# Attention scores of a head pair in TensorE's two row halves, in an attention and MLP kernel

## The chip, the cores and the metric

One core of one Trainium2 chip runs the whole program. The metric is device time in microseconds (us), here the median of several executions. All executions quoted below are in the fast state. "Span" is that of the one execution that was profiled, from its first recorded instruction to its last; it is a little shorter than the time of the same execution (602.1 of 603.85 us in the changed kernel). A first-time reader needs four engine names: TensorE (PE, matmuls, with its weight loads as PEld), VectorE (DVE), ScalarE (ACT) and GpSimd (POOL, which here casts and issues most loads).

## The reference, cut to what matters

```python
q, k, v: (8 batches, 12 heads, 448 positions, 64) float32
q_n = q / (norm(q) + 1e-6);  k_n = k / (norm(k) + 1e-6)
attn = softmax(q_n @ k_n.T / 0.1)              # 448 x 448 per head
x = (attn @ v).transpose(0, 2, 1, 3).reshape(8, 448, 768)
u = x + (x.T @ U @ V).T                        # low rank, 32, along the 448 positions
out = u + relu(u @ w1) @ w2                    # 768 -> 3072 -> 768
```

The two MLP products are most of the arithmetic. The scores contract over 64 dimensions only, but their matmuls use 128 rows of TensorE (`128*128` in the profile), half of them on zeros: that is what the change is about.

## The kernel before

Both kernels are written as a list of operations that a planner puts in order before anything is built, from estimated durations: every engine has a fixed order in the end, and MLP matmuls of one batch are laid between attention matmuls of the next. A changed duration or a changed dependency can therefore move instructions far from the edit.

Before, the two heads' dimensions lie in the two row halves of the transposed array `qkT` (partitions 0 to 63 and 64 to 127). The queries of both heads are used as they lie; the keys of head 0 have zeros in the lower half and those of head 1 zeros in the upper half, so that one K=128 matmul gives the scores of one head. The 2 x 448 keys fill exactly 7 tiles of 128, one of which belongs half to either head. Batch 0's attention, with cuts:

```python
for m in (0, 1, 2, 6, 3, 4, 5) if b == 0 else range(7):
    sc = Slot(r_sc, 1)                                   # one PSUM bank
    nc.tensor.matmul(out=sc.tile[:, 0:S], lhsT=kT[:, 128 * m:128 * (m + 1)],
                     rhs=qkT.tile[:, 8:12, :].rearrange("p c s -> p (c s)"))
    nc.scalar.activation(out=attn.tile[:, m, off:off + S], in_=sc.tile[:, 0:S], func=AF.Exp, scale=inv_tau)
# [cut] then per head: 4 query tiles x 4 key tiles of attn @ [v, 1], 65 columns each
```

The keys must be placed for that: normalised k goes into a 9-block area with zeros around it, 12 blocks are transposed (by TensorE for batches 0 and 1, by a transposing DMA later), three copies per pair rearrange them in batch 0, and v is loaded in pieces that match the mixed tile:

```python
for hh in range(2):
    hs = slice(h0 + hh, h1, 2)
    for j in range(4):
        # [cut] lo, hi, base: which positions of which head go to which partitions of tile j
        for n, c, s0, s1 in segments(lo, hi):            # 98 loads for batches 1 to 7, 8 for batch 0
            nc.gpsimd.dma_start(out=vb[p0:p0 + s1 - s0, hs, j, 0:D],
                in_=v[b, hs].rearrange("h (s c) d -> c s h d", c=SC)[c, s0:s1])
```

The kernel gives out 8 banks of PSUM: three for the MLP and everything else ("mm"), three for scores, two for the products with v ("AV" in the recorded texts).

## Time and profile before

| before | value |
|---|---|
| time | 604.74 us (604.16 to 605.4) |
| span of the profiled execution | 602.4 us |
| TensorE busy | 584.4 us (97%) |
| scores: 336 matmuls of 448 columns | 0.189 us from start to start |
| exps: 336 of 448 columns | 0.439 us from start to start |
| first MLP matmul | 38.69 us after the span's start |

How to read it: from about 45 us on, TensorE nearly always has a matmul to do. Before the first MLP matmul there is nothing to fill TensorE with: the first batch must be loaded, squared, summed, normalised, transposed, scored and put through exp, and several engines take turns in setting the pace. I call that stretch the start. The lines for this are in the prediction below.

### The profile page before, as it was taken

The numbers are of one execution on the slowest core, as the hardware profiler recorded it, in microseconds if no ns is written. First come the engines' busy times: TensorE is split into PE (matmuls) and PEld (weight loads), VectorE is DVE, ScalarE is ACT, GpSimd is POOL, SyncE is SP. The second block draws the span as 40 slices with busy tenths as digits, with TensorE's granted clock in tenths as the row PEclk, the third lists the DMA queues.
The fourth block names the chain that finished last, engine by engine and source line by source line (L and its number), as shares of the span: only waits on it lengthen the run. The fifth ranks groups of instructions, "written<-read, shape, count | busy, mean of one in ns | idle before, by whom it ended". The sixth has DMA issues, their size and how long they took to land.

```text
span 602.4 us, 11513 instructions
## 1 busy us (share of the span) xinstructions
PE 584.4 (97%) x4702; PEld 346.9 (58%) x4725; DVE 300.0 (50%) x722; ACT 278.8 (46%) x604; POOL 114.2 (19%) x175
## 2 busy tenths in 40 slices
PE   4899999999999999999999999999999999999997
PEld 2566766555565665666545666566545666654465
DVE  8979849999998987654721244024300210110011
ACT  7967752577874377316741067505642025014300
POOL 8246334062703406000600000000000000000000
PEclk9999999999999999999999999999999999999999
DMA  9999999999998969715912132030002110310021
GB/s 138 197 181 117 203 202 125 164 135 136 161 167 114 181 104 150 103 56 95 127 20 66 53 73 47 1 93 27 15 1 53 52 40 1 90 41 1 0 53 54
DMA packets 150165, 54.81 MB, mean 91 GB/s; under 512 B 115040, under 2 KB 150112, under 8 KB 150112
## 3 DMA queue, kind: packets, MB, share of 16 engines
q0 software_dynamic: 72864, 25.73, 39.1%
q1 hardware_dynamic: 77184, 28.32, 25.3%
q8 instruction: 37, 0.61, 0.4%
q14 instruction: 16, 0.13, 0.1%
q10 hardware_dynamic: 64, 0.02, 0.0%
HBM read 52.25 MB, written 11.01 MB: 105 GB/s over the span
## 4 chain that ended last, share of the span: by engine, by line
PE 91%; DVE 4%; DMA 2%; ACT 1%; issue 1%; POOL 1%; ACTq 0%; DVEq 0%; POOLq 0%
PE mm L796 36%; PE mm L762 34%; PE sc L572 10%; PE av L594 8%; PE mm L686 1%; DVE xn L536 1%; DMA v_nat<-in_v_dram 1%; DMA qk_nat<-in_q_dram 1%; DVE ss L461 1%; PE tp L374 1%; PE mm L651 1%; ACT attn L577 1%; PE sc L762 0%; POOL qk_nat L396 0%; ACT relu L785 0%
## 5 line engine op out<-in xcount | busy, mean ns | idle before, releaser
L762 PE MATMUL mm<-uT,w_sb 128*128 128x384 bf16 (+1 forms) x1112 | 236.7, 353 | 1.2 <-ACT relu L785 0.2
L796 PE MATMUL mm<-w_sb,relu 128*128 128x384 bf16 (+1 forms) x1368 | 231.9, 324 | 0.3 <-DVE O_sb L805 0.3
L577 ACT ACTIVATE attn<-sc 128x448 bf16<-128x448 f32 x336 | 164.3, 547 | 107.5 <-PE av L594 53.9
L796 PEld LDWEIGHTS <-relu 128*128 128x128 bf16 x1368 | 132.6, 98 | 86.5 <-issue 0.2
L762 PEld LDWEIGHTS <-w_sb 128*128 128x128 bf16 x1152 | 112.1, 98 | 103.9 <-issue 1.4
L785 ACT ACTIVATE relu<-mm 128x512 bf16<-128x512 f32 (+1 forms) x158 | 86.6, 548 | 129.1 <-PE mm L762 128.5
L805 DVE TENSOR_TENSOR O_sb<-mm,u_nat 128x384 f32<-128x384 f32 (+1 forms) x57 | 31.1, 549 | 211.6 <-PE mm L796 208.2
L572 PE MATMUL sc<-qkT 128*128 128x448 bf16 x336 | 104.4, 361 | 3.1 <-ACT attn L577 1.5
L594 PEld LDWEIGHTS <-attn 128*128 128x128 bf16 x1536 | 62.1, 98 | 17.5 <-issue 2.7
L418 POOL DMA_DIRECT2D v_nat<-in_v_dram x98 | 63.2, 654 | 33.2 <-DMA w_sb<-in_moe_w_ch_dram 15.7
L594 PE MATMUL av<-v_nat,attn 128*128 128x65 bf16 x1536 | 66.1, 195 | 0.4 <-DVE X_sb L603 0.2
L461 DVE TENSOR_REDUCE ss<-sq 112x8 f32<-112x512 bf16 x96 | 63.0, 673 | 0.6 <-ACT sq L455 0.4
L536 DVE TENSOR_TENSOR xn<-qk_nat,inv 112x512 bf16<-112x512 bf16 x94 | 60.8, 681 | 0.6 <-DMA qkT<-xn 0.4
L396 POOL DMA_DIRECT2D qk_nat<-in_q_dram x24 | 17.2, 716 | 134.3 <-DVE xn L536 72.9
L603 DVE TENSOR_TENSOR X_sb<-av,rd 128x256 bf16<-128x256 f32 x96 | 40.0, 420 | 1.6
L572 PEld LDWEIGHTS <-qkT 128*128 128x128 bf16 x336 | 28.5, 98 | 20.6 <-issue 5.7
L601 DVE RECIPROCAL rd<-av 128x4 f32<-128x4 f32 x96 | 17.1, 179 | 38.4 <-PE av L594 37.6
L457 DVE TENSOR_TENSOR sq<-qk_nat 112x512 bf16<-112x512 bf16 x89 | 34.2, 413 | 0.5 <-DMA qk_nat<-in_q_dram 0.5
L700 DVE TENSOR_TENSOR u_nat<-mm,X_sb 128x384 bf16<-128x384 f32 x36 | 19.1, 552 | 14.4 <-PE mm L686 14.2
L787 DVE TENSOR_SCALAR relu<-mm 128x384 bf16<-128x384 f32 (+1 forms) x31 | 18.7, 605 | 12.4 <-PE mm L762 11.9
L374 PE MATMUL tp<-ident,xn 112*128 112x112 bf16 x144 | 11.7, 227 | 8.6 <-DVE xn L536 8.2
L474 ACT ACTIVATE ln<-ss 112x32 f32<-112x32 f32 (+2 forms) x26 | 5.9, 228 | 30.3 <-DVE ss L461 30.3
(61 smaller groups left out, 167.8 us busy)
## 6 DMA issues: line engine op xcount, KB each, us to landing
qk_nat<-in_q_dram POOLq DMA_DIRECT2D x23, 224.0 KB, 5.6
qk_nat<-in_k_dram POOLq DMA_DIRECT2D x23, 224.0 KB, 7.0
w_sb<-in_moe_w_ch_dram POOLq DMA_DIRECT2D x4, 1152.0 KB, 14.4
w_sb<-in_moe_w_ch_dram POOLq DMA_DIRECT2D x8, 576.0 KB, 16.2
out_dram<-O_sb SPq DMA_DIRECT2D x15, 168.0 KB, 2.3
out_dram<-O_sb SPq DMA_DIRECT2D x16, 144.0 KB, 2.1
out_dram<-O_sb SPq DMA_DIRECT2D x16, 120.0 KB, 2.0
out_dram<-O_sb SPq DMA_DIRECT2D x16, 96.0 KB, 2.2
```

The source lines that it names most:

```text
L418: nc.gpsimd.dma_start(out=vb[p0:p0 + s1 - s0, hs, j, 0:D], in_=v[b, hs].rearrange("h (s c) d -> c s h d", c=SC)[c, s0:s1]),
L457: nc.vector.tensor_mul(y, x, x)
L461: lambda i=i, a0=a0, a1=a1, sq=sq: nc.vector.reduce_sum(ss.tile[:, i, a0:a1, :].rearrange("p h c -> p (h c)"), sq.tile[:, 0:a1 - a0, :].re ...
L536: nc.vector.tensor_mul(dst, src, sc)
L572: nc.tensor.matmul(out=sc.tile[:, 0:S], lhsT=kT[:, 128 * m:128 * (m + 1)], rhs=qkT.tile[:, 8:12, :].rearrange("p c s -> p (c s)"), start=T ...
L577: exps[m] = plan.add(Op("ACT", act_t(S), lambda sc=sc, m=m: nc.scalar.activation(out=attn.tile[:, m, off:off + S], in_=sc.tile[:, 0:S], fu ...
L594: nc.tensor.matmul(out=av.tile[:, t, 0:D + 1], lhsT=attn.tile[:, m, 128 * t:128 * (t + 1)], rhs=v_t[b % 2][:, h, j, 0:D + 1], start=(j == ...
L603: muls.append(plan.add(Op("DVE", dve_t(256), lambda av=av, rd=rd, h=h: nc.vector.tensor_mul(X.tile[:, :, h * D:(h + 1) * D], av.tile[:, :, ...
L762: o = plan.add(Op("PE", pe_t(n), lambda cc=cc: nc.tensor.matmul(out=mm.tile[:, 0:n], lhsT=w1_sb[:, cc, f * 128:(f + 1) * 128], rhs=uT.tile ...
L785: nc.scalar.activation(out=relu.tile[:, f, 0:n], in_=mm.tile[:, 0:n], func=AF.Relu)
L796: nc.tensor.matmul(out=mm.tile[:, 0:c1 - c0], lhsT=relu.tile[:, f, i * 128:(i + 1) * 128], rhs=w2_t[:, f, c0:c1], start=(f == 0), stop=(f ...
L805: nc.vector.tensor_add(out=O.tile[:, 0:w], in0=mm.tile[:, 0:w], in1=us[i].tile[:, c0:c1]),
```

## The change

The intent: don't stream zeros. Each head needs only 64 rows, so two heads' scores can run at once in the two halves of the array (as measured below, they start 0.003 to 0.004 us apart). Then the keys need no padding, the transposes have 8 blocks instead of 12, one exp can serve both heads (896 columns over two PSUM banks), and v can be loaded with one plain transfer per key tile. Key tiles have 112 keys (448 = 4 x 112). Two tiles are scored in a burst, except in batch 0, where it is one. The PSUM banks become one pool: four for scores in pairs, the other four shared by the rest.

```diff
-        for m in (0, 1, 2, 6, 3, 4, 5) if b == 0 else range(7):
-            sc = Slot(r_sc, 1)
-                nc.tensor.matmul(out=sc.tile[:, 0:S], lhsT=kT[:, 128 * m:128 * (m + 1)],
-                                 rhs=qkT.tile[:, 8:12, :]...)
+        g = 1 if b == 0 else BURST            # BURST = 2
+        for c0 in range(0, SC, g):
+            scs = [Slot(r_sc, 1) for _ in range(g)]
+                for n, sc in enumerate(scs):
+                    for hh in range(2):
+                        r = slice(D * hh, D * hh + D)
+                        nc.tensor.matmul(out=sc.tile[0:SCH, hh, 0:S], lhsT=qkT.tile[r, c0 + n, :],
+                                         rhs=qkT.tile[r, SC:2 * SC, :]...)
-            ... nc.scalar.activation(out=attn.tile[:, m, off:off + S], in_=sc.tile[:, 0:S], ...)
+            ... nc.scalar.activation(out=attn.tile[:, c, :, off:off + S], in_=sc.tile[0:SCH, :, 0:S], ...)
 [cut: load_v, now]
+        ops = [load(lambda c=c: nc.gpsimd.dma_start(
+            out=v_t[b % 2][:, :, c, 0:D], in_=v[b].rearrange("h (s c) d -> c s h d", c=SC)[c]), ...) for c in range(SC)]
 [cut: PSUM]
-    r_mm = ring(3, ...); r_sc = ring(3, ...); r_av = ring(2, ...)
+    r_mm = bank_ring([(7,), (6,), (5,), (4,)], 3)
+    r_av = bank_ring([(4,), (5,), (6,), (7,)], 2, (4, D + 8))
+    r_sc = bank_ring([(0, 1), (2, 3)], 2)
+    r_sc1 = bank_ring([(0,), (2,), (1,), (3,)], 4)
 [cut: no zero fills of xn, no key_tiles copies, 8 blocks instead of 12]
```

## The prediction

> **What bounds the kernel now.** I read the page first: busy shares (part 1), the 40 slices (part 2) and the chain of work that ended last (part 4).
>
> ```profile
> PE 584.4 (97%) x4702; PEld 346.9 (58%) x4725; DVE 300.0 (50%) x722; ACT 278.8 (46%) x604; POOL 114.2 (19%) x175
> ...
> PE   4899999999999999999999999999999999999997
> ...
> DVE  8979849999998987654721244024300210110011
> ACT  7967752577874377316741067505642025014300
> ...
> PE 91%; DVE 4%; DMA 2%; ACT 1%; issue 1%; POOL 1%; ACTq 0%; DVEq 0%; POOLq 0%
> PE mm L796 36%; PE mm L762 34%; PE sc L572 10%; PE av L594 8%; PE mm L686 1%; DVE xn L536 1%; DMA v_nat<-in_v_dram 1%; DMA qk_nat<-in_q_dram 1%; DVE ss L461 1%; PE tp L374 1%; PE mm L651 1%; ACT attn L577 1%; PE sc L762 0%; POOL qk_nat L396 0%; ACT relu L785 0%
> ...
> L577 ACT ACTIVATE attn<-sc 128x448 bf16<-128x448 f32 x336 | 164.3, 547 | 107.5 <-PE av L594 53.9
> ...
> L572 PE MATMUL sc<-qkT 128*128 128x448 bf16 x336 | 104.4, 361 | 3.1 <-ACT attn L577 1.5
> ```
>
> The reader should see that TensorE carries 91% of the chain, and that the scores the change rewrites (L572) are only 10% of it. The two MLP products (L762, L796) are 70% and stay. Because a busy PE need not be a PE at its peak, I also took the start-to-start distances of matmuls. An MLP matmul of 384 columns follows the next by 0.1625 us, one of 512 by 0.216, a score matmul of 448 by 0.189 (the "mean" of 361 ns is a latency that overlaps), an AV matmul of 65 by 0.032. Then the busy time in windows:
>
> ```profile
> 0.00:10.00 10.00, 2.53 (x15) 1.42 (x16) 7.82 (x24) 5.63 (x15) 8.58 (x17) 1.00 0.97 130
> 10.00:20.00 10.00, 7.84 (x60) 4.37 (x59) 9.09 (x23) 9.42 (x24) 4.03 (x6) 1.00 1.67 171
> 20.00:30.00 10.00, 8.41 (x111) 5.28 (x108) 9.77 (x32) 9.35 (x25) 2.99 (x5) 1.00 1.17 203
> ...
> 200.00:250.00 50.00, 50.00 (x461) 31.50 (x460) 40.47 (x97) 31.56 (x73) 17.19 (x26) 1.00 1.10 135
> ```
>
> The columns are PE, PEld, DVE, ACT and POOL busy time, then clock, DMA share, GB/s. So there are two regimes. Up to about 30 us VectorE and ScalarE (9 of 10 us busy) set the pace while the first batch is prepared. After that PE has something to do without a break, because the plan puts MLP matmuls between attention matmuls; any PE time removed there comes off the end, any removed from other engines does not.
>
> [...]No row-tiled matmul is in this trace, but the low-rank product (L651) is column-tiled, and its four starts lie within about 10 ns. [...]this view of PE's timeline shows such a visit:
>
> ```profile
> 150.44 0.38 PE L762 MATMUL mm<-uT,w_sb 128*128 128x512 bf16 x1
> 150.75 0.35 PE L651 MATMUL mm<-X_sb,U_sb 128*32 128x384 bf16 x4
> 151.03 0.55 PE L572 MATMUL sc<-qkT 128*128 128x448 bf16 x2
> 151.42 1.03 PE L762 MATMUL mm<-uT,w_sb 128*128 128x512 bf16 x4
> ```
>
> From 150.44 to 150.75 is 0.31 us where 0.216 is normal: 0.09 to get in. From 150.75 to 151.03 is 0.28 where one 384-column stream takes 0.1625: 0.12 to get out (under 0.01 of it for the three extra starts). The two scores after it lose 0.01 more. A visit to another mode costs about 0.21-0.22 us[...]. [...]Before, all score tiles have 128 columns; after, 112. The trace before has no 112-column load, only 128 columns (98 ns) and 32 columns (92 ns)[...]. This is my main doubt.
>
> **The change part by part.**
> *Scores.* Before, a head pair takes 7 matmuls with 128 keys, K=128 padded with zeros. After, 4 tiles of 112 keys, each as two K=64 matmuls in the row halves at once: 384 matmuls instead of 336, but 192 streams. The order of the changed program has them in 101 runs: 87 runs of two tiles, 12 of one, 2 of three; each run is a visit with its two mode changes. About 17 runs belong to batch 0. For batches 1 to 7, which lie in the PE-bound part: before 294 x 0.189 = 55.6 us; after 168 x 0.190 = 31.9 us of streams plus 84 visits x 0.21 = 17.6 us, sum 49.5. Gain 6.1 us. Of 23.7 us of streams saved, three quarters are given back to mode changes. All of it lies on the path.
> *Transposes on PE* (batches 0 and 1): 8 blocks a pair instead of 12, 48 fewer in all; those of batch 1 are in the PE-bound part: 24 x 0.049 = 1.2 us. In the later batches the transposing DMA moves 8 blocks instead of 12, beside other work: no gain.
> *One exp for two heads.* Back to back the 448-column exp takes 0.439 us, and 512 columns of relu 0.493 against 0.387 for 384: 0.83 ns a column. An exp of 896 columns is then about 0.439 + 448 x 0.00083 = 0.81 us; a pair needs 4 x 0.81 = 3.2 us instead of 7 x 0.439 = 3.1. ScalarE neither gains nor loses; it is half idle after 30 us.
> *Start.* Removed: three copies for the rearranged keys become one. The ScalarE timeline has them as 1.22 us for six in the first pair and 1.03 us for three in later ones; a 448-column copy takes 0.43. That frees about 0.8 + 4 x 0.6 = 3.2 us of ScalarE. VectorE loses a 0.48 us memset at 8.4 us, 0.6 us of memsets of v near 29 us, and 0.4 us in a copy: 1.5 us. The exps add about 0.1 x 5. So 4.2 us of work leave two engines that share it: about 2 us off the start.
> *Loads of v.* 98 + 8 issues become 32, the bytes unchanged. In the start it lets the last q and k load go earlier:
>
> ```profile
> 10.23 0.64 POOL L429 DMA_DIRECT2D v_nat<-in_v_dram  x1 [0.49 <-DMA qk_nat<-in_k_dram]
> 11.60 0.73 POOL L396 DMA_DIRECT2D qk_nat<-in_q_dram  x1 [0.73 <-DMA v_nat<-in_v_dram]
> 12.32 0.70 POOL L396 DMA_DIRECT2D qk_nat<-in_k_dram  x1
> ```
>
> With four v issues that start at 4.66 us, the load now issued at 11.60 goes at about 4.66 + 4 x 0.72 = 7.5. But VectorE waited only 0.51 us for its data, and the queues then carry the same bytes: worth at most that 0.5 us, counted within the 2 us.
> *PSUM.* mm and av shared 5 banks; now they share 4, and scores take 4. With two av banks out, mm has two. An MLP bank is filled in 1.0 to 1.3 us (6 x 0.1625 or 0.216) and emptied in about 0.6, so two should do: 0.
> Sum: 6.1 + 1.2 + 2 = 9.3 us, which would give 595.4.
>
> **Rivals.** *A: the 112-column weight load is slow and shows at each entry.* [...]the total gain is 3.7 and the time 601. [...]Against: no duration of such a load in this trace. *B: in the row-tiled mode the second tile's loads don't hide behind the first, or the two halves load in turn.* Another 0.09 to 0.1 us a visit, 8 us: time 603 with the fast load, 609 together with A. [...]Against: in the trace before, loads for the same rows run under the matmul in flight (the load at 150.04 beside the matmul of 150.04). *C: row halves switch more cheaply than column tiles,* [...]at 0.1 us a visit, 9 us more gain, time 586. Nothing in the trace speaks for it. *D: the four-bank scores or the tighter mm banks make PE wait.* A burst needs both its pairs of banks back from two exps, 1.6 us. Before, PE waited 1.5 us in total on exps; a static order that is wrong by 0.05 us a burst would cost 4 us. Against: MLP matmuls are planned between.
>
> **Range and chances.** Weights: the sum as it stands 0.5, A 0.3, C 0.1, B or D 0.1. Gains 9.3, 3.7, 18, -1: mean 7.5 us. I predict 597.5 us, between the sum and A. The range 589.5 to 603.5 leaves out most of C and the worst of B. A gain over 2% needs a time under 592.6, so a visit cheaper than about 0.18 us or a start shorter by 5: 0.16. Over 2% slower would need a visit above 0.45 us: 0.03. Within 2%: 0.81.
>
> **What would show it.** The distance from the first matmul of a burst to the next MLP matmul: 2 x 0.19 + 0.12, and the one before it longer by 0.09: about 0.59 for a burst in all. [...]if B, the third matmul of a burst starts clearly over 0.19 after the first. The two matmuls of a tile must start within 0.01 us; if they stand 0.19 apart, the halves don't run at once and the whole prediction falls (384 x 0.19 = 73 us of scores). The exps should be near 0.81 us apart, PE's waits still a few us, and the first MLP matmuls some 2 us earlier than before. If the start is unchanged, my step from freed engine time to an earlier start was wrong.

## The result, and the profile after

The changed kernel takes 603.38 us (median of 4; 602.37 to 605.72) against 604.73 us for the kernel before in the same rounds (4; 604.16 to 605.4). The ratio is 0.998, with a 95% interval of 0.9958 to 1.0002. Ratios here are the mean time of one kernel's fast runs over that of the other's of the same rounds, so not quite the ratio of the medians quoted. The time lies at the upper end of the predicted range, but a gain of 7 us was forecast, and 1.35 us were measured, which the interval doesn't tell from nothing. Also new: the executions spread over 3.4 us, where those of the kernel before spread over 1.2.

The page of the changed kernel: busy shares, TensorE's 40 slices, the chain that ended last by engine and by line, and two of its groups (all PSUM tiles are now called "bank"; L587 is the scores, L593 the exps, L607 the product with v, L775 and L809 the MLP):

```profile
PE 580.7 (96%) x4704; PEld 329.7 (55%) x4725; DVE 311.0 (52%) x728; ACT 271.1 (45%) x425; POOL 75.2 (12%) x101
...
PE   3799999999999999999999999999999999999997
...
PE 92%; DVE 4%; DMA 1%; POOL 1%; issue 1%; ACT 0%; DVEq 0%; POOLq 0%
PE bank L775 36%; PE bank L809 36%; PE bank L587 8%; PE bank L607 8%; DMA qk_nat<-in_q_dram 1%; PE bank L699 1%; PE bank L443 1%; DVE xn L553 1%; PE bank L664 1%; POOL v_nat L472 1%; DVE u_nat L713 1%; POOL qk_nat L463 0%; DVE u_nat L710 0%; DVE relu L800 0%; ACT attn L593 0%
...
L593 ACT ACTIVATE attn<-bank 112x896 bf16<-112x896 f32 x192 | 166.8, 915 | 132.1 <-PE bank L587 87.4
...
L587 PE MATMUL bank<-qkT 64*112 64x448 bf16 x384 | 61.4, 390 | 4.0 <-ACT attn L593 3.4
```

The reader sees the scores fall from 10% of the chain to 8%, which is a gain, and TensorE's first two slices of 15 us go from 4 and 8 tenths to 3 and 7, which is a loss: TensorE comes to work later. Both regimes have changed, in opposite directions.

**The stretch that TensorE bounds.** A burst in TensorE's timeline of the changed kernel (start, busy time of the group, line, shape, count):

```profile
201.82 1.18 PE L607 MATMUL bank<-v_nat,attn 112*128 112x65 bf16 x32
202.93 0.59 PE L587 MATMUL bank<-qkT 64*112 64x448 bf16 x4
203.45 1.31 PE L809 MATMUL bank<-w_sb,relu 128*128 128x384 bf16 x7
```

From the burst's first start to the next MLP start are 0.52 us. Taken apart with the starts of single instructions, over the 84 bursts of batches 1 to 7: the entry costs 0.093 us more than the normal distance; the two halves of a tile start 0.003 to 0.004 us apart, so they do run at once; the second tile starts 0.230 us after the second half of the first; the next matmul starts 0.282 us after the second tile, 0.093 more than its 0.189 of streaming. Sum: 0.093 + 0.006 + 0.230 + 0.282 = 0.611 us for what took 3.5 x 0.189 = 0.662 before (half of a pair's 7 matmuls). That is 0.05 us a burst, 4.2 us in all, where I had 6.1.

**The start.** The first MLP matmul comes at 42.83 us instead of 38.69: 4.1 us later, where I had expected 2 us earlier. Busy time by engine (PE, PEld, DVE, ACT, POOL, then clock, DMA share, GB/s) in three windows, first before, then after:

```profile
20.00:25.00 5.00, 3.90 (x52) 2.43 (x50) 4.93 (x14) 4.41 (x13) 0.97 (x1) 1.00 1.25 222
25.00:30.00 5.00, 4.52 (x60) 2.85 (x58) 4.84 (x19) 4.94 (x13) 2.02 (x4) 1.00 1.08 184
30.00:35.00 5.00, 4.94 (x87) 3.48 (x88) 2.81 (x10) 4.58 (x11) 5.00 (x8) 1.00 1.09 132
```

```profile
20.00:25.00 5.00, 3.81 (x35) 2.41 (x36) 4.82 (x11) 3.49 (x9) 1.04 (x1) 1.00 1.29 215
25.00:30.00 5.00, 5.00 (x47) 3.09 (x44) 3.85 (x10) 4.02 (x7) 4.59 (x7) 1.00 1.20 191
30.00:35.00 5.00, 4.18 (x58) 2.94 (x56) 1.65 (x6) 4.08 (x6) 3.92 (x5) 1.00 1.14 171
```

VectorE and ScalarE are relieved, as I had counted (3.85 against 4.84, 4.02 against 4.94 in the middle window), but nothing comes sooner for it: TensorE is busy for all of 25 to 30 us and gets through only 47 matmuls. TensorE's timeline says why:

```profile
22.30 1.16 PE L443 MATMUL bank<-ident,xn 112*128 112x112 bf16 x8 [0.84 <-DVE xn L553]
23.39 0.99 PE L587 MATMUL bank<-qkT 64*112 64x448 bf16 x4
24.31 1.94 PE L607 MATMUL bank<-v_nat,attn 112*128 112x65 bf16 x32
```

The 32 products with v take 1.94 us here and 1.18 at 201.82: 54 ns from start to start instead of 32; the transposes of 112 columns likewise start 93 ns apart here and 49 in the later ones. That is TensorE at half its clock: where later runs put matmuls of 384 columns into the start, these begin 0.320 us apart before the clock rises and 0.1625 after, and warm_after's windows below print a granted clock of 0.50. The trace's clock records begin with full clock at 32.4 us in this execution, and at 18.7 us in that of the kernel before. The windows above nevertheless print a clock of 1.00, because the record shows nothing for the time before its first entry: here the spacing of known matmuls must be read, not the clock column. Of the first 20 us, TensorE was busy for 8.64 in the changed kernel and for 10.37 in the kernel before; what busy share lifts the clock is not shown.

A second thing in the same stretch, from the chain of waits before, then after:

```profile
11.60 4.89 DMA qk_nat<-in_q_dram
...
19.16 2.40 DVE xn L536 x4
...
24.74 2.50 DVE xn L536 x4
...
29.46 0.22 DVE v_nat L842
...
30.02 0.27 PE av L594 x3
```

```profile
8.36 8.24 DMA qk_nat<-in_q_dram
...
19.66 3.20 DVE xn L553 x4
22.90 0.56 PE bank L443 x4
...
24.38 1.88 PE bank L607 x32
...
33.07 0.93 ACT attn L593
```

The last load of q and k is now issued at 8.36 us instead of 11.60 and lands at the same 16.5 to 16.6: the fewer issues of v bring nothing. And the same four normalisations take 3.20 us of the chain instead of 2.40. Then the two chains part: before, VectorE carries the chain from 16.6 to 30.0 us, one of the removed memsets of v among it; after, it hands over to TensorE at 22.9 us, which carries the chain at half clock until an exp takes over at 33.07.

The account so far. In both kernels exactly batch 0's attention lies before the first MLP matmul. From there to the end of TensorE's last matmul the kernel before takes 560.31 us and the changed one 555.83, 4.5 us less; with the start's +4.1 that is the -0.3 measured between the two spans (602.4 and 602.1). Of the 4.5, scores give 4.2 and the transposes of batch 1 1.2 (24 fewer, as predicted); TensorE's waits after 45 us are about 1.8 us before and 2.1 after. So 0.6 us are not accounted for. (The traces show 3.1 and 4.1 us of idle time there, but 1.3 and 2.0 of it stand where two or three weight loads are recorded between two matmuls, which are places where the record of a matmul is missing. castx below, with no such place, has 2.1.) Why the burst costs more and why the start got longer is what the experiments are for.

### The profile page after: what moved, and what is told of

The parts are those of the page before. It is cut to its first block, busy times and chain, and to the rows that moved or that the text cites. A ratio compares the mean times of both kernels' runs of the same rounds, so it can differ in the third digit from the quotient of the medians.

```text
span 602.1 us, 11326 instructions
## 1 busy us (share of the span) xinstructions
PE 580.7 (96%) x4704; PEld 329.7 (55%) x4725; DVE 311.0 (52%) x728; ACT 271.1 (45%) x425; POOL 75.2 (12%) x101
## 4 chain that ended last, share of the span: by engine, by line
PE 92%; DVE 4%; DMA 1%; POOL 1%; issue 1%; ACT 0%; DVEq 0%; POOLq 0%
PE bank L775 36%; PE bank L809 36%; PE bank L587 8%; PE bank L607 8%; DMA qk_nat<-in_q_dram 1%; PE bank L699 1%; PE bank L443 1%; DVE xn L553 1%; PE bank L664 1%; POOL v_nat L472 1%; DVE u_nat L713 1%; POOL qk_nat L463 0%; DVE u_nat L710 0%; DVE relu L800 0%; ACT attn L593 0%
## 5 line engine op out<-in xcount | busy, mean ns | idle before, releaser
L775 PE MATMUL bank<-uT,w_sb 128*128 128x384 bf16 (+1 forms) x1132 | 230.6, 352 | 3.3 <-issue 1.4
L809 PE MATMUL bank<-w_sb,relu 128*128 128x384 bf16 (+1 forms) x1368 | 231.2, 323 | 0.6 <-DVE O_sb L818 0.3
L593 ACT ACTIVATE attn<-bank 112x896 bf16<-112x896 f32 x192 | 166.8, 915 | 132.1 <-PE bank L587 87.4
L809 PEld LDWEIGHTS <-relu 128*128 128x128 bf16 x1368 | 129.3, 98 | 91.5 <-issue 12.2
L775 PEld LDWEIGHTS <-w_sb 128*128 128x128 bf16 x1152 | 108.0, 98 | 111.0 <-issue 18.5
L798 ACT ACTIVATE relu<-bank 128x384 bf16<-128x384 f32 (+1 forms) x136 | 74.4, 547 | 131.7 <-PE bank L775 131.4
L587 PE MATMUL bank<-qkT 64*112 64x448 bf16 x384 | 61.4, 390 | 4.0 <-ACT attn L593 3.4
L607 PEld LDWEIGHTS <-attn 112*128 112x128 bf16 x1536 | 57.9, 99 | 11.6 <-issue 4.6
L607 PE MATMUL bank<-v_nat,attn 112*128 112x65 bf16 x1536 | 61.1, 196 | 0.2 <-DVE uT L841 0.2
L800 DVE TENSOR_SCALAR relu<-bank 128x384 bf16<-128x384 f32 (+1 forms) x56 | 34.3, 613 | 32.0 <-PE bank L775 30.1
L616 DVE TENSOR_TENSOR X_sb<-bank,rd 128x256 bf16<-128x256 f32 x96 | 39.2, 418 | 1.5
L614 DVE RECIPROCAL rd<-bank 128x4 f32<-128x4 f32 x96 | 16.6, 178 | 42.7 <-PE bank L607 42.0
L472 POOL DMA_DIRECT2D v_nat<-in_v_dram x32 | 29.8, 941 | 51.8 <-PE bank L607 51.5
L587 PEld LDWEIGHTS <-qkT 64*112 64x112 bf16 x384 | 18.8, 128 | 26.9 <-issue 23.1
## 6 DMA issues: line engine op xcount, KB each, us to landing
w_sb<-in_moe_w_ch_dram POOLq DMA_DIRECT2D x8, 576.0 KB, 16.6
```

Source lines behind the costliest of these rows:

```text
L472: ops = [load(lambda c=c: nc.gpsimd.dma_start(out=v_t[b % 2][:, :, c, 0:D], in_=v[b].rearrange("h (s c) d -> c s h d", c=SC)[c]), SCH * H ...
L587: nc.tensor.matmul(out=sc.tile[0:SCH, hh, 0:S], lhsT=qkT.tile[r, c0 + n, :], rhs=qkT.tile[r, SC:2 * SC, :].rearrange("p c s -> p (c s)"), ...
L593: exps.append(plan.add(Op("ACT", act_t(2 * S, 0.08), lambda sc=sc, c=c0 + n: nc.scalar.activation(out=attn.tile[:, c, :, off:off + S], in_ ...
L607: nc.tensor.matmul(out=av.tile[:, t, 0:D + 1], lhsT=attn.tile[:, j, hh, 128 * t:128 * (t + 1)], rhs=v_t[b % 2][:, h, j, 0:D + 1], start=(j ...
L616: muls.append(plan.add(Op("DVE", dve_t(256), lambda av=av, rd=rd, h=h: nc.vector.tensor_mul(X.tile[:, :, h * D:(h + 1) * D], av.tile[:, :, ...
L775: o = plan.add(Op("PE", pe_t(n), lambda cc=cc: nc.tensor.matmul(out=mm.tile[:, 0:n], lhsT=w1_sb[:, cc, f * 128:(f + 1) * 128], rhs=uT.tile ...
```

## The experiments

Theory S (start): the start got longer because TensorE runs at half clock in it and other engines wait for it. Rivals: a slower exp chain on ScalarE; a collision of VectorE with GpSimd's cast. Theory B (burst): what is missing in the bursts is the mode change and the 112-column weight load; rival: waits for the shared PSUM banks. Fifteen kernels ran; all are correct but the one that was meant to be wrong.

| run | edit to | time (range, n) | ratio to before, 95% | first MLP at |
|---|---|---|---|---|
| warm_after | after | 602.51 (601.14-602.75, 5) | 0.9967, 0.9955-0.998 | 41.77 |
| warm_before | before | 606.05 (605.13-606.82, 9) | 1.0029, 1.0019-1.0039 | 38.79 |
| burst1 | after | 614.86 (614.65-615.45, 4) | 1.0178, 1.0164-1.0192 | 41.76 |
| key128 | after | 599.83 (599.07-599.96, 5) | 0.9924, 0.9911-0.9938 | 41.32 |
| hot | after | 602.89 (600.93-603.52, 5) | 0.9966, 0.9952-0.9979 | 43.34 |
| castlate | after | 602.32 (600.5-605.71, 5) | 0.9973, 0.995-0.9997 | 41.28 |
| expsplit | after | 602.45 (600.91-603.09, 4) | 0.9963, 0.9949-0.9976 | 41.52 |
| hot_cast_key128 | after | 600.44 (599.76-601.74, 5) | 0.9935, 0.9923-0.9947 | 42.80 |
| hot2 | after | 601.53 (601.33-602.05, 5) | 0.9958, 0.9946-0.997 | 40.34 |
| castx | after | 601.7 (600.26-605.53, 14) | 0.9963, 0.995-0.9977 | 40.31 |
| hot2_castx | after | 601.52 (601.1-602.54, 5) | 0.9958, 0.9946-0.997 | 40.73 |
| hot2_castx_key128 | after | 598.69 (598.18-599.8, 5) | 0.991, 0.9897-0.9923 | 41.11 |
| castx_exphalf (wrong on purpose) | after | 600.32 (599.52-601.45, 4) | 0.9929, 0.9912-0.9945 | 40.42 |
| castx_key128 | after | 598.87 (598.4-599.3, 4) | 0.9909, 0.9894-0.9924 | 40.53 |
| castx_key128_b0 | after | 602.25 (601.91-603.28, 6) | 0.9968, 0.9956-0.998 | 43.67 |

"First MLP at" is that of the one profiled execution, and one execution says little when they spread over 3 us. But what follows the first MLP matmul hardly varies: to TensorE's last matmul, the profiled executions of castlate, hot2, castx and castx_exphalf take 555.83 to 555.86 us, where the changed kernel took 555.83. So among these runs a difference of time is a difference of the start, and medians over all executions can be compared. castlate turned out to be the changed kernel's program again (see there), which makes nine executions of it: median 602.92 us (600.5 to 605.72). By the same constant rest (603.85 - 42.83 = 561.02 us beside the start), that is a first MLP matmul at about 41.9 us, so the usual loss in the start is about 3 us rather than 4.1. The kernel before had medians of 604.1 to 604.4 in all these rounds.

### Burst length: burst1

One tile a visit in all batches. If the mode change is what costs, halving the tiles per visit must show it.

```diff
-    BURST = 2
+    BURST = 1
```

> The changed kernel with one key tile a burst instead of two in all batches: 158 visits to the row-tiled mode instead of 101. Theory (a visit costs a fixed 0.093 us in and 0.093 us out beside its streams): two visits of one tile take 2 x 0.379 = 0.758 us where one of two takes 0.611, so 57 x 0.147 = 8 us more, total about 611.5 us, no new waits. Rival (visits are hidden and the missing gain went into waits for PSUM banks and exps): no change or a small gain, 601 to 604 us.

Measured: 614.86 us, 11.5 us over the changed kernel. TensorE's timeline:

```profile
215.91 0.65 PE L809 MATMUL bank<-w_sb,relu 128*128 128x384 bf16 x3
216.50 0.40 PE L587 MATMUL bank<-qkT 64*112 64x448 bf16 x2
216.82 0.66 PE L809 MATMUL bank<-w_sb,relu 128*128 128x384 bf16 x3
```

Three MLP matmuls at 0.1625 would let the next one start at 215.91 + 0.49 = 216.40; the visit starts at 216.50, so 0.10 to get in, and 0.32 passes until the MLP goes on, 0.137 more than one stream of 448. A single-tile visit thus takes 0.422 us, and what it replaces, 1.75 of the old matmuls, took 0.331. There are 141 visits after 45 us instead of 84, and all their entries, tiles and exits add up to 64.8 us against 51.4 (84 x 0.611), 13.4 more; from the first MLP matmul to TensorE's last this run takes 568.12 us instead of 555.83, 12.3 more. I had expected 8 because I had put the exit at 0.093 after one tile too. Theory B holds for the mode change; TensorE's waits after 45 us did not grow (1.3 us of idle time). Why the exit costs more after a single tile is open.

### Width of the weight load: key128

Load 128 key columns instead of 112 (16 of them belong to the next block; their score rows are computed into rows that nothing reads). Streams and visits stay; only the weight load, and the rows written, get wider.

```diff
-   nc.tensor.matmul(out=sc.tile[0:SCH, hh, 0:S], lhsT=qkT.tile[r, c0 + n, :], ...)
+   k0 = SCH * (c0 + n)
+   nc.tensor.matmul(out=sc.tile[:, hh, 0:S], lhsT=qkT.tile[r].rearrange("p b s -> p (b s)")[:, k0:k0 + 128], ...)
```

> The changed kernel with 128 columns in each key load instead of 112 (the 16 more are the next block's first columns, and the scores of these rows are not read). Theory [...]: the second tile of a burst starts 0.19 to 0.20 us after the first instead of 0.230, perhaps a shorter entry too: 84 x 0.035 = 3 us less, 600 us. Rival (a load for rows that a matmul is using waits in the row-tiled mode, whatever its columns): 0.230 us stays, 603 us.

Measured: 599.83 us, 3.55 below the changed kernel's median. A burst, in its timeline:

```profile
199.35 1.18 PE L609 MATMUL bank<-v_nat,attn 112*128 112x65 bf16 x32
200.47 0.55 PE L588 MATMUL bank<-qkT 64*128 64x448 bf16 x4
200.95 1.31 PE L811 MATMUL bank<-w_sb,relu 128*128 128x384 bf16 x7
```

The burst takes 0.48 us to the next MLP start instead of 0.52: the second tile follows the first by 0.196 us instead of 0.230, and entry (0.096) and exit (0.282) stay. 84 x 0.034 = 2.9 us. The loads of one burst by their records, the changed kernel first (count, then shortest, median and longest in ns, then first and last start in us):

```profile
L587 PEld LDWEIGHTS <-qkT x4: 123/124/126, 202.9 to 203.0; 64*112 64x112 bf16 x4
```

```profile
L588 PEld LDWEIGHTS <-qkT x4: 92/94/95, 200.5 to 200.5; 64*128 64x128 bf16 x4
```

Here 128 columns load faster than 112: 94 ns against 124. So my doubt about the 112-column load was right, but it doesn't show where I put it. The entry is the same for both widths; it is the second tile that is late. Its loads start under the first tile's streams (at 202.98, when the first tile has been running since 202.93 and, at 0.189 us a stream, goes on until 203.12), so they are pulled ahead. By their records they also end before that, at 203.10, and yet the second tile starts only at 203.16: the records don't show where the 0.04 us go, only that 0.034 of it goes with the wider load. Nor does the entry follow the length of the load: it stays at 0.093 to 0.096 us while the load takes 124 or 94 ns. I did not take the wider output rows apart from the wider load. Of the 3.55 us, 2.5 lie after the first MLP matmul (553.36 us to TensorE's last instead of 555.83); the rest is the start, which varies from execution to execution.

### Is it the exps, in the steady part: expsplit

Two exps of 448 columns per tile, as many instructions as the old form would have needed.

```diff
-   nc.scalar.activation(out=attn.tile[:, c, :, ...], in_=sc.tile[0:SCH, :, 0:S], ...)
+   # [cut: the bank counts one more use]
+   for hh in range(2):
+       nc.scalar.activation(out=attn.tile[:, c, hh, ...], in_=sc.tile[0:SCH, hh, 0:S], ...)
```

> The changed kernel with one exp for each head again (448 columns instead of 896). Theory (ScalarE off the path after 30 us): eight exps of 0.439 us a pair instead of four of 0.835, 3.5 against 3.3 us, hidden behind TensorE; total within 1.5 us of the changed kernel's 603.4. Rival (an exp of 0.84 us keeps the relus behind it waiting and TensorE with them): 2 to 3 us faster, and fewer waits of the MLP matmuls for their banks.

Measured: 602.45 us, within its own spread of the changed kernel, and 556.21 us from the first MLP matmul on against 555.83, though ScalarE had more to do. The exps don't bound the steady part. (The fused exp itself is 0.835 us from start to start, where I had estimated 0.81.)

### TensorE's clock: warm_after, warm_before, hot, hot2

Matmuls on a constant tile, whose results nobody reads, keep TensorE busy in the gaps. In warm_after and its control warm_before, 60 of them are planned with low priority at the very start:

```diff
+    for w_ in range(60):
+        plan.add(Op("PE", 0.33 if w_ < 12 else 0.17, lambda wm=wm: nc.tensor.matmul(
+            out=wm.tile[:, 0:384], lhsT=warm_t[:, 0:128], rhs=warm_t), ...), pe_warm)
```

> The changed kernel with 60 dummy matmuls of 384 columns that the plan puts where it expects TensorE to be idle in the first 35 us (they write a free PSUM bank; the result stays right). Theory (the start lost 4 us because TensorE ran at half clock until 32 us instead of 20 us): AV matmuls 32 ns apart instead of 54 ns in the stretch from 15 to 32 us, first MLP matmul at about 38 to 39 us instead of 42.8, total about 599 us. Rival (the start is later because of the order of the work, the data landing at 16.6 us or ScalarE, and the slow clock is only a symptom): the clock rises early but the first MLP matmul stays at 42 to 43 us, total 603 us.

> The kernel before with the same dummy matmuls, as a control. Clock theory: it was slow only until about 19 us, where VectorE sets the pace, so little is to be had: first MLP matmul at 37.5 to 38.7, total 603.5 to 605. If dummy matmuls help both kernels by the same 4 us, the later start of the changed kernel is not explained by the clock.

Measured: warm_before 606.05 us, 0.3% slower than before although its clock is up at 4.2 us: before, the clock was no hindrance. warm_after 602.51 us, which is less than I had expected of it. Its windows show what went wrong, and here the clock column can be believed, since a record had begun:

```profile
15.00:20.00 5.00, 2.21 (x31) 1.64 (x30) 3.75 (x9) 3.99 (x8) 0.29 (x1) 0.90 1.25 230
20.00:25.00 5.00, 4.21 (x43) 2.87 (x42) 4.33 (x10) 4.09 (x9) 1.03 (x1) 0.50 1.29 214
25.00:30.00 5.00, 5.00 (x65) 3.19 (x62) 4.52 (x12) 3.65 (x6) 3.89 (x6) 0.92 0.98 154
```

The clock was up at 5.4 us, and TensorE, busy for 2.2 of 5 us from 15 to 20, lost it again at 19.0, for the stretch where it matters. About 3.3 us of dummies stood on the path besides. So I tried to place them better.

> The changed kernel with dummy matmuls of 384 columns forced into the first 25 us: 22 at the very start, one to three after each score burst of the first three pairs, two ahead of each group of transposes of the third and fourth pair (the first dummies left TensorE slow again from 19 to 26 us). Theory (about half of the later start is the slow clock): the clock stays up from about 5 us on, AV matmuls 32 ns apart from the first, first MLP matmul at 39 to 40.5 us, total 600.5 to 601.5. Rival (the start is bounded by ScalarE's exps and VectorE, the clock does not matter): first MLP matmul at 41.5 or later although the clock is up, total 602 to 603 us.

> The changed kernel, its plan and order untouched, with dummy matmuls only where TensorE stands still anyway: 22 before the first transposes, 10 before the second pair's last score burst (which waits for exps until 18.3 us), 3 before two groups of transposes that wait for VectorE. The runs with planned dummies mixed two things, the clock and dummies on the path. Clock theory: clock up from about 6 us to the end, AV matmuls 32 ns apart in the whole start, first MLP matmul at 39.5 to 40.5 us (41.3 to 41.8 with the clock up at 27 us, 42.8 at 32 us), total about 601. Rival (with the clock up the start then waits for ScalarE and VectorE): 41 us or later.

In hot (22 dummies first, then some planned after the bursts of the first pairs) the planned dummies changed the plan's order, and the first MLP came at 43.34 us, later than ever: inconclusive. In hot2 the dummies were given to the instruction stream without the planner's knowledge, so the order stayed:

```diff
+    # [cut] 22 before the first transposes, 10 before pair 1's last scores, 3 before two later transposes
+    dummies(tp.group[0], dup)
```

Measured: 601.53 us, with a spread of only 0.7 us (601.33 to 602.05) against 3.4 for the changed kernel; the clock was still lost from 11.8 to 18.6 us, but full from then on, and the first MLP came at 40.34. The cast still met a normalisation in it (1.48 us), so this is the clock alone: 1.4 us between its median and that of the nine executions of the changed kernel. The clock is real, but it is about half of the loss, not all. Theory S as I had put it is too big. It may also be behind the spread: over the profiled executions without dummies the clock rises anywhere between 25.7 and 32.4 us, and the latest rise came with one of the latest first MLPs. That is not shown, since key128 spreads over only 0.9 us without dummies.

### VectorE against GpSimd's cast: castlate, castx

In the changed kernel's timelines, VectorE's four normalisations, and GpSimd's cast of V:

```profile
19.57 3.27 DVE L553 TENSOR_TENSOR xn<-qk_nat,inv 112x512 bf16<-112x512 bf16 x4
```

```profile
20.65 1.04 POOL L870 CAST V_sb<-raw_uv 128x448 bf16<-128x448 f32 x1 [2.90 <-DMA raw_uv<-in_moe_V_dram]
```

The cast falls into the middle of the four; the one it meets takes 1.47 us instead of 0.68. Before, the same cast ran at 22.57 us (0.97 us) and met a reduction (0.67 us), a copy (0.38), two reciprocals (0.17 and 0.15) and the start of a product (0.43), and none of them took over 0.01 us longer than its like. To move it, castlate added dependencies to the cast:

```diff
-   plan.add(Op("POOL", 1.2, cast_v, deps=v0 + [z], rel=[uv]), pool_q),
+   plan.add(Op("POOL", 1.2, cast_v, deps=v0 + [z] + muls0[1:], rel=[uv]), pool_q),
```

> The changed kernel with GpSimd's cast of the low-rank V held back until the first pair's products are done. In the changed kernel one normalisation on VectorE took 1.47 us instead of 0.68 while this cast of 1.04 us ran on GpSimd, in the kernel before no normalisation met it. Theory (the two disturb each other, and the normalisation is on the start's chain): the normalisation at 20.8 us takes 0.68, the first MLP matmul comes up to 0.8 us earlier, total about 602.6. Rival (chance, or not on the chain): nothing changes, 603.4 us.

Measured: 602.32 us (600.5 to 605.71), but the trace shows the cast still on a normalisation (1.46 us). The edit did not reach the program: the instructions of the two traces, shapes included, are the same on every engine, in the same order. So this run tests nothing, but it gives five more executions of the changed kernel. castx instead makes GpSimd really wait, with a one-element copy of the first result of attention ahead of the cast:

```diff
+   nc.gpsimd.tensor_copy(out=gate, in_=X0.tile[0:1, 0, D:D + 1])
    nc.gpsimd.tensor_copy(out=V_sb[:, PAD:PAD + S]..., in_=V_f()...)
```

> The changed kernel, its order untouched, with GpSimd's cast of V held back by a one-element copy that reads the first pair's second product (castlate only changed the plan's numbers: on the chip the cast still met a normalisation). Theory: no normalisation takes 1.47 us any more, the third pair's q and k are ready 0.8 us earlier and the first MLP matmul comes about 0.5 to 0.8 us earlier, total about 602.5. Rival: VectorE's 0.8 us is taken up by later waits, no change.

The same two lines for castx:

```profile
19.16 2.48 DVE L553 TENSOR_TENSOR xn<-qk_nat,inv 112x512 bf16<-112x512 bf16 x4
```

```profile
23.34 0.98 POOL L873 CAST V_sb<-raw_uv 128x448 bf16<-128x448 f32 x1
```

The four take 2.48 us again, 0.8 less, TensorE's order is the same as in the changed kernel, and the first MLP comes at 40.31 us. The median of 14 executions is 601.7 us, 1.2 below that of the changed kernel's nine (1.7 below that of the four first), with a range as wide (600.26 to 605.53). The clock rose at 25.7 us here, against 26.4 in castlate and 27.3 in key128, so part of this may be the clock. A second pair of runs says the same: castx_key128 below differs from key128 by the held-back cast alone, and its median is 1.0 us lower (598.87 against 599.83; four and five executions). The collision is shown, and is worth about 1 us.

### The parts together: hot_cast_key128, hot2_castx, hot2_castx_key128, castx_key128

The first had all three ideas in their planned forms.

> All three together: key loads of 128 columns, TensorE kept warm in the start, the cast held back. If the causes add up (3.5 us from the loads, 2 to 3 from the clock, up to 0.8 from the cast): 597 to 598 us. If the start is bounded elsewhere, no better than the loads of 128 columns alone, 599.8 us.

Measured: 600.44 us, not better than key128 alone: the cast collided again and the order changed. A miss.

> Both. If they explain the later start, the first MLP matmul is at 38.7 to 39.7 us as in the kernel before (38.7), total about 600 us. If it stays at 40.5 or later with the clock up and no long normalisation, the rest of the later start is the new order of exps and scores itself.

> Both with key loads of 128 columns: 3 us less again (84 bursts x 0.034), 597 us if the start comes back fully, and faster than both kernels.

> The changed kernel with key loads of 128 columns and the cast held back, no dummies. If the two add up (3.5 us and 1 to 1.7 us below 603.4): 598 to 599 us and first MLP matmul at about 40.2 us, faster than both kernels by about 1%. If the cast's gain was chance: 599.8 us like the loads alone.

Measured: hot2_castx 601.52 us, no better than either part. In its profiled execution the data of q and k landed some 0.9 us later, and ten dummies stood on the path for 2.6 us (0.26 us each, where full clock has 0.1625), and the moved cast met another normalisation (1.07 us), so the parts don't simply add. With the wider load, hot2_castx_key128 has 598.69 and castx_key128 598.87 us, which can't be told apart; castx_key128 needs no dummies and is the version I would keep: 5.3 us (0.9%) faster than the kernel before, and 4.5 faster than the change as it stood.

### What is left of the start: castx_exphalf, castx_key128_b0

With the cast out of the way the first MLP still comes 1.6 us later than before. castx_exphalf, wrong on purpose (relative error 0.25), lets the exps of batch 0 do half their columns from the third pair on:

```diff
-   out=attn.tile[:, c, :, off:off + S], in_=sc.tile[0:SCH, :, 0:S]
+   out=attn.tile[:, c, :, off:off + (S // 2 if b == 0 and p > 1 else S)],
+   in_=sc.tile[0:SCH, :, 0:S // 2 if b == 0 and p > 1 else S]
```

> castx with the exps of the first batch's last four pairs over half their columns (a wrong result on purpose, same order, same TensorE work). Theory (from 24 us on ScalarE's exps set the pace of the start: 16 x 0.835 = 13.4 us where the kernel before had 28 x 0.439 = 12.3): the exps take 0.46 us, the first MLP matmul comes from 40.3 to 38.5 us or earlier, and the total falls by as much, to about 600. Rival (TensorE's or VectorE's order sets it): first MLP matmul stays within 0.5 us of 40.3.

Measured: the first MLP at 40.42 us, no earlier; but this execution came later to the end of the second pair (26.04 us against 24.81). The stretch from there to the first MLP, as busy times, for castx, for castx_exphalf and for the kernel before:

```profile
24.81:40.31 15.50, 13.86 (x205) 9.16 (x202) 9.37 (x28) 13.30 (x19) 8.74 (x12) 1.00 1.17 180
```

```profile
26.04:40.42 14.38, 13.40 (x204) 8.83 (x202) 9.27 (x28) 8.98 (x19) 9.00 (x12) 1.00 1.19 180
```

```profile
26.58:38.69 12.11, 11.57 (x187) 7.84 (x186) 8.93 (x35) 10.80 (x26) 7.35 (x11) 1.00 1.08 164
```

In castx two engines are nearly full in this stretch: TensorE (13.86 of 15.50) and ScalarE (13.30). Relieving ScalarE by 4.3 us shortens it by only 1.1; then TensorE is nearly full alone (13.40 of 14.38). The times say more than this one profile, which is of the slowest of four executions: the median is 600.32 us (599.52 to 601.45), about the 600 of the theory and 1.4 below castx's. So the exps do set part of the pace, as far as four executions whose range overlaps with castx's can show it.

The third line is not the same work. At its start the kernel before had done 24 of the batch's 42 score matmuls, castx only 10 of its 24 tiles. The 14 tiles left stand for 24.5 old matmuls, where the kernel before had 18 left: 6.5 x 0.189 = 1.2 of TensorE's 1.8 us more are scores that were not made ahead. The 14 tiles come in nine visits of one tile (0.422 us each, by burst1), one of two (0.611) and one of three (0.84, an estimate: 0.611 + 0.233), together 5.25 us against 24.5 x 0.189 = 4.63. So the visits themselves cost some 0.6 us. As a remedy I made the visits of batch 0 two tiles long, from the second pair on:

```diff
-        g = 1 if b == 0 else BURST
+        g = 1 if b == 0 and p == 0 else BURST
 [cut: the same condition where qkT's uses are counted]
```

> castx_key128 with two tiles a burst in the first batch too, from its second pair on (92 visits of two tiles in all, one of one, and three longer runs or merged ones). Theory (one-tile visits make TensorE the bound of the late start): about 10 visits fewer, 0.2 us each, so the first MLP matmul at about 38.5 to 39 us instead of 40.5, total about 597. Rival (ScalarE's exps, 0.835 us each without a gap from 24 to 38 us, hold the start where it is, and the coarser bursts make them wait): 40.5 us or later, total 599 or more.

Measured: 602.25 us, 3.4 slower than castx_key128, first MLP at 43.67, as the rival had it. A line of ScalarE's timeline and one of TensorE's:

```profile
32.37 3.34 ACT L595 ACTIVATE attn<-bank 112x896 bf16<-112x896 f32 x4 [1.17 <-PE bank L588]
```

```profile
33.34 0.37 PE L588 MATMUL bank<-qkT 64*128 64x448 bf16 x2 [0.82 <-ACT attn L595]
```

ScalarE waits 1.17 us for scores, and TensorE 0.82 us for an exp. A burst of two needs both double banks, and there are only two: no scores can be made while the exps of the last burst run. Shorter visits were the cheaper evil, and my remedy fell. That the single-tile visits cost 0.6 us in the start is therefore argued from the sum, not shown; a test would need more banks for scores in the start, and the kernel has given out all eight. Some of the start stays open.

## Why the prediction was right or wrong

**Scores (predicted 55.6 to 49.5 us, gain 6.1): mechanism right, size too large.** The halves of a tile start 0.003 to 0.004 us apart, and a visit costs 0.233 us beyond its streams, where I had 0.21 from the column-tiled product. The gain was 4.2. Of the rivals, B has the right sign in part: the second tile was late, at 0.230 instead of 0.189, 0.041 and not 0.09 to 0.1; A named the right cause, the 112-column load (124 against 94 ns), but put it at the entry, which is the same 0.093 to 0.096 for both widths; the size I gave it, a total gain of 3.7, was an assumption that no run shows. key128 gets 0.034 of the 0.041 back. C, a cheaper switch, is refuted; so is D in the steady part: TensorE's waits went from about 1.8 to 2.1 us. What sets the price stays open: the entry is the same for loads of 124 and 94 ns.

**Transposes (1.2), PSUM (0), ScalarE's exps (neither gain nor loss in the steady part): right.** The exp of 896 columns is 0.835 us instead of my 0.81.

**Start (predicted 2 us earlier): this is the step that failed.** I wrote "So 4.2 us of work leave two engines that share it: about 2 us off the start." The work did leave them, and the start grew by about 3 us (4.1 in the profiled execution). Part of the work had been on the path, which ran over VectorE until 30.0 us; but in the changed kernel the path leaves VectorE at 22.9 us, and other engines set the pace. Four things stand in place of the step. (1) The collision of the cast with a normalisation, about 1 us, shown by castx and by castx_key128 against key128. (2) TensorE's clock, which I had not looked at, since the page printed full clock: full at 25.7 to 32.4 us instead of 18.7; about 1.4 us, by hot2. (3) The exps in a row on ScalarE from the third pair on, about 1.4 us by the medians of castx_exphalf and castx: with one exp for two heads, 16 x 0.835 = 13.4 us stand against 28 x 0.439 = 12.3. (4) TensorE's own time in single-tile visits, about 0.6 us, argued. They overlap and don't add: castx with hot2 gains no more than either.

**Loads of v (at most 0.5 within the 2):** nothing. The load issued 3.2 us earlier landed at the same time, as I had suspected when I wrote that the queues carry the same bytes.

In sum: -4.5 us from the first MLP matmul on, and about +3 in the start (with the -1.35 measured between the medians, 3.1), in place of -7.3 and -2. My check for it was on record ("If the start is unchanged, my step from freed engine time to an earlier start was wrong"), and it gave the answer at first sight; the ways in which a start could grow were in none of the rivals.

## What to carry to other kernels

Count a change of TensorE's tiling mode as a price per visit (here 0.233 us beyond its streams for two tiles, against 0.189 for a whole 448-column matmul), make visits long where the banks allow it (one tile took 0.422 us, two 0.611; in the start, longer visits made the kernel 3.4 us slower), and try full 128-column weights even if some of them are thrown away (here a load took 94 ns for 128 columns and 124 for 112). In a stretch that several engines pace in turn, don't credit freed engine time as time saved: follow which result each engine waits for, and what the freed engine will now run into. Compare starts by the times of all executions, if the rest is as constant as here (555.83 to 555.86 us), and not by one profile. And read TensorE's clock from the spacing of a known matmul in a start (here 54 and 32 ns for 65 columns), before trusting a column that has no record yet.
